# A retention layer and a mixture of experts on one core: the short last chunk as full-array matmuls, and a new order of the first tile

## The chip, the cores and the metric

The kernel runs on one core of one Trainium2 chip. The metric is the device time of one launch in microseconds (us). Most executions of a kernel agree within 0.3%. Every run lists its span and its mean granted TensorE clock, where 1.0 is full speed. A ratio is the mean time of one kernel's fast runs over that of the other's of the same rounds, with a 95% interval, so it is not quite the ratio of the medians that are quoted beside it.

PE is the matmul engine, DVE is VectorE, ACT is ScalarE, POOL is GpSimd, SP is the engine whose queue issues most DMAs. L514 is line 514 of the kernel that was profiled; the two kernels' line numbers differ.

## The reference, cut to what matters

```python
# attention without softmax, per batch (8) and head (8): seq 576, head_dim 64
scores = scale * (q @ k.T)                     # 576 x 576
ret    = scores * gamma[h] ** (i - j)          # for i >= j, else 0
attn   = ret @ v
# x: (8*576, 512) = (4608, 512); then four experts
for e in range(4):
    out += p[:, e:e+1] * (relu(x @ w1[e]) @ w2[e])     # w1: 512x1024, w2: 1024x512
```

576 positions are four chunks of 128 and a short last chunk of 64, called the remainder. The experts take x in nine tiles of 512 rows. Tile 0 holds most of batch 0, tile 1 the remainder of batch 0 and most of batch 1, and so on. While PE works on the experts of tile t, the attention of batch t+1 is woven in between.

## The kernel before

One tile of the experts is a generator. It gives way after each group of matmuls: eight "up" groups of four 512-column matmuls and four "down" groups of eight, for each of four experts, 48 steps numbered from 0. A plan says what attention work follows which step.

```python
def moe(nt, lead=0):
    for e in range(E):
        for fc in range(NFC):                       # 8 up groups
            # for e == 0 and fc < lead: columns 0..255 early, the rest here
            up(ph, e, fc, slice(0, NT)); nc.scalar.activation(hT[:, fc, :], ph, Relu)
            yield
        for ns in range(NSUB):                      # 4 down groups
            ...                                     # po += hT x w2; acc += probs * po
            yield
```

Two heads sit in one pair, on partitions 0 to 63 and 64 to 127. Scores and values of the remainder use two 64x64 corners of the array for each pair:

```python
def Srem(self):
    for p in range(NP):                             # 4 pairs of heads
        for j in (0, 64):
            r = slice(j, j + 64)
            nc.tensor.matmul(s[r, p, :], lhsT=self.qkT[r, 1, p, SM:S], rhs=self.qkT[r, 0, p, SM:S], ...)
# in O_values, if rem: the same loop with lhsT = self.r["v"][r, p, :], rhs = self.sT["r"][r, p, :]
```

The start: after the attention of batch 0, the weights are queued on POOL, and the loads of the remainder and of all later batches stand on SP behind a wait for the first down weights.

```python
load_w1(0, 0); load_w1(0, 1)        # first expert's up weights, in halves, earlier
w20 = load_w2(0)                    # first down weights
for e in range(1, E): load_w1(e); load_w2(e)
load_rem(0, w20)                    # on SP: starts when w20 has landed
load_chunk(1, 0); load_chunk(1, 1)  # and all further loads behind it, in order
```

Batch 1 is transposed on PE in tile 0 (`Tc`, steps 40, 42, 44, 46). From batch 2 on, q and k are transposed by DMA. On SP the loads of batch 2, the four output stores of tile 0 and the ten DMA transposes of batch 2 stand in this order; the transposes read what POOL has cast. The plan for these tiles:

```python
at(7 if nt == 1 else 0, begin)                           # casts, then dmaT(c), then load(b + 1)
at(19 if nt == 1 else 17, lambda: state["A"].S([0, 1]))  # first scores of the next batch
at(24, ... Srem, O_values([0, 1]), kv_all, kv_sum, Srem_mask)
```

## Time and profile before

| | before |
|---|---|
| time, median of the three runs at the start | 561.4 us (560.63 to 562.08) |
| span of the profiled run | 559.2 us |
| PE busy | 98% |
| expert matmuls | 2304 of 512 columns, 216 ns from start to start: 497 us |

PE is the bottleneck, so every pause of PE costs time, unless a later wait of PE becomes shorter by as much. DMA is the second one, for about the first 97 us. The page says so. Its first line gives busy time by engine, the other two lines are 40 equal slices of 14 us: the DMA engines' busy share in tenths, and what they moved.

```profile
PE 545.6 (98%) x3469; PEld 262.5 (47%) x3530; DVE 165.7 (30%) x283; ACT 217.0 (39%) x371; POOL 109.8 (20%) x182
...
DMA  9999999591369025910594058803300100010001
GB/s 232 176 203 200 209 206 231 104 213 15 104 131 180 1 84 89 217 28 38 109 179 92 0 123 157 135 1 98 63 2 1 73 3 0 1 76 0 1 0 75
```

The waits view of PE lists who waited for whom: total us, times, longest.

```profile
PE pt L437 <- POOL qm L427: 2.3, 3, 1.0
PE po L543 <- DMA wt_492<-in_moe_w_dram: 1.7, 1, 1.7
...
PE ph L514 <- DVE xT L329: 0.8, 1, 0.8
```

The first is start-up. The second is the wait for the first down weights at 26 us. The third is the start of tile 1, which needs the last chunk of batch 1.

The timeline of PE in tile 1 has the remainder's scores (start, us, engine, line, count):

```profile
115.02 1.03 PE L514 MATMUL ph<-xT,wt_504 128*128 128x512 bf16 x4
115.97 0.31 PE L336 MATMUL sr<-qkT 64*64 64x64 bf16 x8
116.21 0.64 PE L351 MATMUL o<-sT,vm 128*64 128x128 bf16 x16
```

The last expert matmul of the first line started at 115.66, and the next matmul could have started 216 ns later; it started 309 ns later. Counted the same way, pauses of 92 to 99 ns stand at the changes of the array's form (128x128, 128x64, 64x128, 64x64) in tiles 1 to 6 of this trace. The Trainium skill says that changing the tiling mode drains the engine ("TensorEngine Tiling (Array Packing)", "Key Properties"); it gives no figure, and these 93 ns are one that this case shows.

Last, SP's timeline for the transposes of batch 2 (each with the time its issue took), and PE's timeline for the scores that need them.

```profile
92.28 2.94 SPq L552 DMA_DIRECT2D out_dram<-acc  x4
95.83 1.32 SPq L268 DMA_TRANSPOSE qkT<-qm  x1
...
102.42 1.26 SPq L268 DMA_TRANSPOSE qkT<-km  x1
...
105.04 1.26 SPq L268 DMA_TRANSPOSE qkT<-km  x1
```

```profile
100.54 7.07 PE L514 MATMUL ph<-xT,wt_500 128*128 128x512 bf16 x31
107.55 0.23 PE L276 MATMUL s_1438<-qkT 64*128 64x128 bf16 x1
...
107.72 0.22 PE L276 MATMUL s_1438<-qkT 64*128 64x128 bf16 x1
```

The last k transpose is issued at 105.04 us. The trace's landings of the k transposes before and after it are 2.4 to 2.7 us after their issue, so it lands near 107.5 to 107.7. The first matmul that reads it is the seventh one, at 107.72. PE does not wait there, but it has next to no slack.

### The profile page before, as it was taken

How to read it: one execution, taken by the hardware profiler on the slowest of the kernel's cores; microseconds unless marked ns; L12 is line 12 of the kernel's file. 1: busy time of each engine (PE TensorE's matmuls, PEld its weight loads, DVE VectorE, ACT ScalarE, POOL GpSimd, SP SyncE). 2: the span in 40 equal slices, each digit the busy share in tenths (PEclk: the TensorE clock that was granted, in tenths of full speed). 3: DMA queues.
4: the chain of work that ended last, by engine and by line, in shares of the span. 5: the costliest groups of instructions: out<-in, count | busy, mean ns of one | idle time of the engine just before them, and what ended most of it. 6: DMA issues, size and time to landing. Idle time of an engine off the chain costs nothing.

```text
span 559.2 us, 8453 instructions
## 1 busy us (share of the span) xinstructions
PE 545.6 (98%) x3469; PEld 262.5 (47%) x3530; DVE 165.7 (30%) x283; ACT 217.0 (39%) x371; POOL 109.8 (20%) x182
## 2 busy tenths in 40 slices
PE   7899999999999999999999999999999999999997
PEld 4544455454445444444445444544444444444443
DVE  5402262253214520462035212542046202220222
ACT  6442344433353235323433334323532353335332
POOL 7611247026001520044002600250010000000000
PEclk9999999999999999999999999999999999999999
DMA  9999999591369025910594058803300100010001
GB/s 232 176 203 200 209 206 231 104 213 15 104 131 180 1 84 89 217 28 38 109 179 92 0 123 157 135 1 98 63 2 1 73 3 0 1 76 0 1 0 75
DMA packets 148277, 53.83 MB, mean 96 GB/s; under 512 B 130668, under 2 KB 142188, under 8 KB 148240
## 3 DMA queue, kind: packets, MB, share of 16 engines
q1 hardware_dynamic: 141296, 44.79, 39.2%
q0 software_dynamic: 6800, 8.39, 8.8%
q8 instruction: 27, 0.44, 0.4%
q10 hardware_dynamic: 144, 0.13, 0.1%
q14 instruction: 10, 0.08, 0.1%
HBM read 45.16 MB, written 9.44 MB: 98 GB/s over the span
## 4 chain that ended last, share of the span: by engine, by line
PE 94%; DMA 3%; POOL 1%; issue 1%; SPq 1%; DVE 0%
PE po L543 44%; PE ph L514 43%; DMA wt_492<-in_moe_w_dram 2%; PE o L351 1%; DMA raw_k<-in_k_dram 1%; PE o L365 1%; SPq L85 1%; POOL km L423 0%; PE sr L336 0%; PE orem L358 0%; PE ptc L297 0%; POOL wt_269 L125 0%; PE kvb L389 0%; PE kva L389 0%; PE oc L322 0%
## 5 line engine op out<-in xcount | busy, mean ns | idle before, releaser
L533 ACT ACTIVATE hT<-ph 128x512 bf16<-128x512 f32 x288 | 171.6, 597 | 274.6 <-PE ph L514 274.6
L543 PEld LDWEIGHTS <-hT 128*128 128x128 bf16 x1160 | 112.5, 98 | 134.6 <-DMA wt_492<-in_moe_w_dram 2.2
L549 DVE SCALAR_TENSOR_TENSOR acc<-po,probs,acc 128x512 f32<-128x512 f32 (+1 forms) x109 | 81.3, 746 | 234.6 <-PE po L543 226.8
L514 PE MATMUL ph<-xT,wt_504 128*128 128x512 bf16 x280 | 66.3, 379 | 0.5
L514 PE MATMUL ph<-xT,wt_269 128*128 128x512 bf16 (+1 forms) x303 | 64.2, 362 | 1.4 <-DVE xT L329 0.8
L543 PE MATMUL po<-wt_492,hT 128*128 128x512 bf16 x286 | 63.4, 379 | 1.8 <-DMA wt_492<-in_moe_w_dram 1.7
L543 PE MATMUL po<-wt_506,hT 128*128 128x512 bf16 x273 | 63.8, 379 | 0.8
L514 PE MATMUL ph<-xT,wt_500 128*128 128x512 bf16 x280 | 64.1, 379 | 0.5
L543 PE MATMUL po<-wt_510,hT 128*128 128x512 bf16 (+1 forms) x287 | 63.4, 373 | 0.5
L514 PE MATMUL ph<-xT,wt_508 128*128 128x512 bf16 x286 | 63.7, 379 | 0.2 <-issue 0.2
L543 PE MATMUL po<-wt_502,hT 128*128 128x512 bf16 x280 | 63.4, 379 | 0.4
L403 POOL CAST sbd<-ksum 64x256 bf16<-64x256 f32 x36 | 14.4, 399 | 221.2 <-DVE ksum L408 197.6
L514 PEld LDWEIGHTS <-wt_269 128*128 128x128 bf16 x312 | 30.0, 98 | 32.1 <-issue 0.9
L514 PEld LDWEIGHTS <-wt_508 128*128 128x128 bf16 x288 | 28.0, 98 | 33.3
L514 PEld LDWEIGHTS <-wt_500 128*128 128x128 bf16 x288 | 27.7, 98 | 33.4
L514 PEld LDWEIGHTS <-wt_504 128*128 128x128 bf16 x288 | 26.9, 98 | 30.3
L547 ACT ACTIVATE acc<-po,probs 128x512 f32<-128x512 f32 x36 | 24.7, 687 | 40.1 <-PE po L543 39.1
L235 POOL TENSOR_TENSOR km<-raw_k,gk 128x512 bf16<-128x512 f32 x28 | 29.2, 1043 | 13.9 <-DMA raw_k<-in_k_dram 9.5
L237 POOL CAST vm<-raw_v 128x512 bf16<-128x512 f32 x28 | 17.3, 616 | 41.8 <-PE o L351 34.9
L237 POOL CAST qm<-raw_q 128x512 bf16<-128x512 f32 x28 | 17.1, 611 | 7.4 <-DMA raw_q<-in_q_dram 7.2
L374 DVE TENSOR_TENSOR xT<-o,gq 128x512 bf16<-128x512 f32 x24 | 15.5, 686 | 7.6 <-PE o L365 7.6
L240 POOL TENSOR_TENSOR krb<-raw_kr,gk 64x512 bf16<-64x512 f32 x8 | 8.3, 1037 | 13.8 <-DMA raw_kr<-in_k_dram 13.2
(231 smaller groups left out, 238.7 us busy)
## 6 DMA issues: line engine op xcount, KB each, us to landing
out_dram<-acc SPq DMA_DIRECT2D x35, 256.0 KB, 2.0
raw_k<-in_k_dram SPq DMA_DIRECT2D x32, 256.0 KB, 5.0
raw_q<-in_q_dram SPq DMA_DIRECT2D x32, 256.0 KB, 5.1
raw_v<-in_v_dram SPq DMA_DIRECT2D x32, 256.0 KB, 5.2
wt_269<-in_moe_w_dram POOLq DMA_DIRECT2D x2, 512.0 KB, 5.6
wt_492<-in_moe_w_dram POOLq DMA_DIRECT2D x1, 1024.0 KB, 11.7
wt_500<-in_moe_w_dram POOLq DMA_DIRECT2D x1, 1024.0 KB, 14.5
wt_502<-in_moe_w_dram POOLq DMA_DIRECT2D x1, 1024.0 KB, 20.4
```

The costliest lines, as they stand in the source:

```text
L85: nc.sync.dma_start(out=pairs_of(state[b][n, hf])[:, h], in_=src[b, h, 256 * hf:256 * hf + 256, :].rearrange("h (p j) d -> p h (j d)", j=2))
L235: eng.tensor_tensor(o, i, gk[:, c, :].unsqueeze(2).to_broadcast([128, H, D]), op=MULT)
L237: eng.tensor_copy(o, i)
L240: eng.tensor_tensor(self.r["k"], self.t["kr"], gk[:R, NCH, :].unsqueeze(2).to_broadcast([R, H, D]), op=MULT)
L351: nc.tensor.matmul(o[64 * j:64 * j + 64, c * C:(c + 1) * C], lhsT=self.m["v"][:, c, 2 * p + j, :], rhs=self.sT[p][:, j, c, :], start=(c == ...
L374: nc.vector.tensor_tensor(xT[:, p, b * S:b * S + SM], o, gq[:, p, 0:SM], op=MULT)
L403: eng.tensor_copy(sbd[r, n, :, r], src[r])
L514: nc.tensor.matmul(ph[:, ts], lhsT=w1_sb[e][:, dc, fc * 128:(fc + 1) * 128], rhs=xT[:, dc, n0 + ts.start:n0 + ts.stop], start=(dc == 0), s ...
L533: nc.scalar.activation(hT[:, fc, :], ph, Relu)
L543: nc.tensor.matmul(po, lhsT=hT[:, fc, ns * 128:(ns + 1) * 128], rhs=w2_sb[e][:, fc, d:d + w], start=(fc == 0), stop=(fc == NFC - 1))
L547: nc.scalar.activation(a, po, Copy, scale=pe)
L549: nc.vector.scalar_tensor_tensor(a, po, pe, a, op0=MULT, op1=ADD)
```

## The change

It has two parts. First, the remainder's k (transposed) and v are put into block-diagonal 128x128 operands, so that one full-array matmul does a pair of heads and the array keeps its form. Second, tile 0 runs up 0, up 1, down 0, down 1 instead of up 0, down 0, up 1, down 1, so that the first down weights are needed later; the second expert's up weights are therefore loaded before them, in halves, and the remainder of batch 0 moves to later steps. Some smaller parts go with it: the transposed mixing probabilities move into the start-up, the transposes of batch 1 come one step earlier (39, 41, 43, 45), and tile 1's early part stops at column 384, before the last chunk of batch 1.

```diff
+    kbd = const.tile([128, NP, 128], BF16)          # zeroed once, also the warm-up operand
+    vbd = const.tile([128, NP, 128], BF16)
 # cast_rem
-            for n in ("q", "v"):
-                eng.tensor_copy(self.r[n], self.t[n + "r"])
+            eng.tensor_copy(self.r["q"], self.t["qr"])
+            for j in (0, 64):
+                eng.tensor_copy(vbd[j:j + 64, :, j:j + 64], self.t["vr"][j:j + 64])
+        def put_krem(self, eng, src):
+            for j in (0, 64):
+                eng.tensor_copy(kbd[j:j + 64, :, j:j + 64], src[j:j + 64])
 # Srem
-                for j in (0, 64):
-                    r = slice(j, j + 64)
-                    nc.tensor.matmul(s[r, p, :], lhsT=self.qkT[r, 1, p, SM:S], rhs=self.qkT[r, 0, p, SM:S], ...)
+                nc.tensor.matmul(s[:, p, :], lhsT=kbd[:, p, :], rhs=self.qkT[:, 0, p, SM:S], start=True, stop=True)
 # values of the remainder: from O_values (64x64) to O_states (lhsT=vbd[:, p, :]), next to the state matmuls
 # moe(): ups(e) and downs(e) are generators of their own
+        first = [ups(0), ups(1), downs(0), downs(1)] if nt == 0 else [ups(0), downs(0), ups(1), downs(1)]
-    tiles = [moe(nt, lead=3 if nt < 2 else 0) for nt in range(n_nt)]
+    tiles = [moe(0, lead=3, pause=True), moe(1, lead=2, cut=3 * NT // 4)] + [moe(nt) for nt in range(2, n_nt)]
 # start
+    load_w1(1, 0)
+    load_w1(1, 1)
+    late_constants()
     w20 = load_w2(0)
-    late_constants()
-    for e in range(1, E):
+    load_w2(1)
+    for e in range(2, E):
 # plan of tile 0: remainder of batch 0 at 29, 31, 36 instead of 20, 22, 24
-            for c, g in enumerate((40, 42, 44, 46)):
+            for c, g in enumerate((39, 41, 43, 45)):
 # plan of tiles 1 to 6
+            at(20, lambda: state["A"].put_krem(nc.gpsimd, state["A"].qkT[:, 1, :, SM:S]))
 # ... cut: transposed_probs() split off, ksum with 3 buffers instead of 4, identf earlier; Sc(3), Oc(3) of batch 1
#     moved from behind tile 0 into its plan
```

More of the change, by code (lines that the diff above doesn't have):

```diff
@@ L133 @@
     load_paired(0)
-    warm_in = const.tile([128, 512], BF16)
-    nc.vector.memset(warm_in, 0.0)
+    kbd = const.tile([128, NP, 128], BF16)
+    nc.vector.memset(kbd, 0.0)
     def warm(n):
@@ L139, in warm @@
         for _ in range(n):
-            nc.tensor.matmul(warm_out, lhsT=warm_in[:, 0:128], rhs=warm_in, start=True, stop=True)
+            nc.tensor.matmul(warm_out, lhsT=kbd[:, 0, :], rhs=kbd[:, :, :].rearrange("p a i -> p (a i)"), start=True, stop=True)
     probs_raw = const.tile([NTT, 128, E], FP32)
@@ L156 @@
     make_identity(nc, ident)
+    identf = const.tile([NTT, NTT], FP32)
+    nc.gpsimd.tensor_copy(identf, ident[:NTT, :NTT])
     tri2 = const.tile([128, 2, 128], BF16)
@@ L163 @@
     tri = const.tile([128, 128], BF16)
-    identf = const.tile([NTT, NTT], FP32)
     trir = const.tile([128, R], BF16)
@@ L176, in late_constants @@
                                 base=0, channel_multiplier=-1, pattern=[[1, 128]])
-        nc.gpsimd.tensor_copy(identf, ident[:NTT, :NTT])
     lgp = const.tile([128, NP], FP32)
@@ L199, with transposed_probs @@
     nc.vector.memset(sbd, 0.0)
+    vbd = const.tile([128, NP, 128], BF16)
+    nc.vector.memset(vbd, 0.0)
     probs = const.tile([128, E, NTT], FP32)
     psm = const.tile([128, NTT], FP32)
-    def mixing_weights():
-        pp = ps_at.tile([128, E, NTT], FP32, tag="at", name="pp")
+    def transposed_probs():
+        pp = ps_mm.tile([128, E, NTT], FP32, tag="mm", name="pp")
         for e in range(E):
@@ L207, in mixing_weights @@
         nc.vector.tensor_copy(probs, pp)
+    def mixing_weights():
         nc.vector.tensor_reduce(psm, probs[:, :, :].rearrange("p e t -> p t e"),
@@ L227, in __init__ @@
             self.r = {n: att1.tile([R, H, D], BF16, tag=n + "r", name=n + "rb") for n in "kq"}
-            self.r["v"] = att1.tile([128, NP, D], BF16, tag="vr", name="vrb")
             self.qkT = att1.tile([128, 2, NP, S], BF16, tag="qkT")
@@ L261, in Trem @@
                     nc.tensor.transpose(pt[:, i, p, :], flat(self.r[n][:, 2 * p:2 * p + 2, :]), ident[:R, :R])
-            nc.vector.tensor_copy(self.qkT[:, :, :, SM:S], pt)
+            nc.vector.tensor_copy(self.qkT[:, 0, :, SM:S], pt[:, 0])
+            self.put_krem(nc.vector, pt[:, 1])
+        def put_krem(self, eng, src):
+            for j in (0, 64):
+                eng.tensor_copy(kbd[j:j + 64, :, j:j + 64], src[j:j + 64])
         def dmaT(self, c):
@@ L333, in Srem @@
             for p in range(NP):
-                for j in (0, 64):
-                    r = slice(j, j + 64)
-                    nc.tensor.matmul(s[r, p, :], lhsT=self.qkT[r, 1, p, SM:S], rhs=self.qkT[r, 0, p, SM:S],
-                                     start=True, stop=True, skip_group_check=True)
+                nc.tensor.matmul(s[:, p, :], lhsT=kbd[:, p, :], rhs=self.qkT[:, 0, p, SM:S], start=True, stop=True)
             self.srem = s
@@ L353, in O_values @@
                                          start=(c == 0), stop=False, skip_group_check=True)
-            if rem:
-                for p in range(NP):
-                    for j in (0, 64):
-                        r = slice(j, j + 64)
-                        nc.tensor.matmul(self.orem[r, p, :], lhsT=self.r["v"][r, p, :], rhs=self.sT["r"][r, p, :],
-                                         start=(p == 0), stop=False, skip_group_check=True)
         def O_states(self, pairs, rem=False):
@@ L368, in O_states @@
             if rem:
+                for p in range(NP):
+                    nc.tensor.matmul(self.orem[:, p, :], lhsT=vbd[:, p, :], rhs=self.sT["r"][:, p, :],
+                                     start=(p == 0), stop=False, skip_group_check=True)
                 for n in self.rem_states:
@@ L393, in kv_sum @@
         def kv_sum(self):
-            ksum = att1.tile([128, NCH, NP, D], FP32, tag="ksum", name="ksum")
+            ksum = att1.tile([128, 3, NP, D], FP32, tag="ksum", name="ksum")
             parts = [self.kvp[n // 2][:, n % 2] for n in range(NCH)]
@@ L407, in kv_sum @@
             for n in range(1, NCH):
-                nc.vector.tensor_tensor(ksum[:, n], ksum[:, n - 1], parts[n], op=ADD)
-                put(nc.gpsimd, ksum[:, n], n)
+                nc.vector.tensor_tensor(ksum[:, n % 3], ksum[:, n - 1], parts[n], op=ADD)
+                put(nc.gpsimd, ksum[:, n % 3], n)
     class AttP(Att):
@@ L506, in O, with moe @@
                                         gq[:, 2 * u:2 * u + 2, ts], op=MULT)
-    def moe(nt, lead=0):
+    def moe(nt, lead=0, cut=NT // 2, pause=False):
         n0 = nt * NT
@@ L517, in moe, with ups @@
         acc = [apool.tile([128, Dm], FP32, tag="acc", name="acc") for _ in range(NSUB)]
-        for e in range(E):
-            hT = hpool.tile([128, NFC, NT], BF16, tag="hT")
-            for fc in range(NFC):
-                if e == 0 and fc < lead:
-                    if fc == 0:
-                        early = [ps_mm.tile([128, NT], FP32, tag="mm", name="ph") for _ in range(lead)]
-                        for x in range(lead):
-                            up(early[x], e, x, slice(0, NT // 2))
-                            if x != 1:
-                                yield
+        hTs = {}
+        def ups(e):
+            hT = hTs[e] = hpool.tile([128, NFC, NT], BF16, tag="hT", name="hT")
+            n = lead if e == 0 else 0
+            early = [ps_mm.tile([128, NT], FP32, tag="mm", name="ph") for _ in range(n)]
+            for x in range(n):
+                up(early[x], e, x, slice(0, cut))
+                if pause and x != 1:
+                    yield
+            for fc in range(NFC):
+                if fc < n:
                     ph = early[fc]
-                    up(ph, e, fc, slice(NT // 2, NT))
+                    up(ph, e, fc, slice(cut, NT))
                 else:
@@ L534, in moe, with downs @@
                 yield
+        def downs(e):
+            hT = hTs[e]
             for ns in range(NSUB):
@@ L553, in moe @@
                 yield
+        first = [ups(0), ups(1), downs(0), downs(1)] if nt == 0 else [ups(0), downs(0), ups(1), downs(1)]
+        for stage in first + [g for e in range(2, E) for g in (ups(e), downs(e))]:
+            yield from stage
     a0 = AttP(0)
     UNITS = [(hf, u) for hf in range(2) for u in range(2)]
-    tiles = [moe(nt, lead=3 if nt < 2 else 0) for nt in range(n_nt)]
+    tiles = [moe(0, lead=3, pause=True), moe(1, lead=2, cut=3 * NT // 4)] + [moe(nt) for nt in range(2, n_nt)]
     tile0 = tiles[0]
@@ L581 @@
         a0.kv(hf, u)
+    transposed_probs()
     next(tile0)
@@ L604 @@
             at(3, lambda: a0.cast_rem(nc.gpsimd))
-            at(20, a0.Trem)
-            at(22, a0.Srem, a0.Srem_mask)
-            at(24, a0.Orem)
+            at(29, a0.Trem)
+            at(31, a0.Srem, a0.Srem_mask)
+            at(36, a0.Orem)
             def begin1():
@@ L619 @@
             at(25, begin1)
-            for c, g in enumerate((40, 42, 44, 46)):
+            for c, g in enumerate((39, 41, 43, 45)):
                 at(g, lambda c=c: state["a1"].Tc(c))
-                if c < 3:
-                    at(g + 1, lambda c=c: state["a1"].Sc(c))
+                at(g + 1, lambda c=c: state["a1"].Sc(c))
                 if c > 0:
@@ L626 @@
                 at(g + 1, lambda c=c: state["a1"].kv(c))
+            at(47, lambda: state["a1"].Oc(3))
         elif nt + 1 < B:
@@ L654 @@
                 f()
-        if nt == 0:
-            state["a1"].Sc(3)
-            next(tiles[1])
-            next(tiles[1])
-            state["a1"].Oc(3)
 _INS = ['q', 'k', 'v', 'moe_domain_probs', 'moe_w1', 'moe_w2']
```

## The prediction

> **What bounds the kernel now.** Span 559.2 us. The page gives PE 98% busy, and the chain of work that ended last is 94% PE, nearly all expert matmuls. Their starts in the timeline are 216 ns apart at 512 columns, the warm spacing that the Trainium skill gives ("TensorE: Matmul & The Clock Gate", "Wait — 56ns, not 53.3ns?": 215.7 ns). 2304 of them are about 497 us, so some 62 us are attention, start-up and waits. PE's waits (waits view) are few: 1.7 us for the first down weights (timeline: 26.25 to 27.99), 0.8 us for xT at the start of tile 1, some 2.8 us in the start-up.
>
> **What the change removes, by the timeline's starts.**
> - Short chunk: eight 64x64 matmuls sit between pauses of about 93 ns, paid when PE changes its array form. Amid expert matmuls the scores cost 337 ns; four full-array 64-column ones should cost 4x29 ns (the spacing of the state matmuls now). Estimate: 0.21 us saved for scores and 0.22 for values in batches 0 and 1. In batches 2 to 7 other tiled matmuls are adjacent and one pause remains: 551 to 435 ns for scores, about the same for values: 0.24 us a batch, 1.45 us in all.
> - Tile 0 as up, up, down, down: the 1.74 us wait goes. The second expert's up weights (2 x 2.9 us after 20.4) come just in time; the first down weights then land at 33 to 34 us, where PE needs them at about 33: 0 to 1 us of wait left.
> - Tile 1's early part stops at 384 columns, so it no longer waits for the last chunk of batch 1: 0.78 us. The transposed probabilities fill an idle gap: 0.3 us.
>
> **What it adds.** POOL makes the block-diagonal k copies and one more v copy; it is 20% busy and off the chain.
>
> **Why little of it will arrive.** DMA is saturated to about 97 us (page, slices). The loads of batches 1 and 2 are gated by the first down weights, which now land 5 us later, so this queue loses 5 us of sharing (27 GB/s, the gain of slices 28 to 70 us over 14 to 28): about 0.6 us later. Two places wait for it:
> 1. In tile 0 the transposes of batch 1 come one step earlier, while its chunks land as before (q of chunk 1 at 67.3, of chunk 2 at 71.3 us): 1 to 2 us of new waits.
> 2. In tile 1 the scores of batch 2 start at 107.55 us. Their last DMA transpose is issued at 105.04 and lands, by its neighbours' 2.5 us, at 107.5: no slack. PE should come there 2 to 3 us earlier and wait until about 108.1. What was won before this point is swallowed.
>
> Later tiles have about 5 us of slack there (scores at 165.5, landing 160.5), so their 1.45 us stays. Sum: +0.5 - 1.45, about -1 us.
>
> **Predicted: 560.4 us, 8 in 10 within 558.2 to 561.9. Faster by over 2%: 0.02; within 2%: 0.97; slower: 0.01.**
>
> **What would show it.** Waits view: under 1 us for the first down weights; none for xT at tile 1; new waits for POOL's casts in the transposes of batch 1, and 2 to 3 us for the DMA transposes in the first scores of tile 1. Timeline: short-chunk scores 29 ns apart; tiles 2 to 7 of 59.45 us instead of 59.69.
>
> **What would make it wrong.** If the loads come no later, or the transposes of tile 1 start earlier, up to 5 us arrive (556 us). If PE's clock drops in the new wait, it is slower by about 1 us.

## The result, and the profile after

| | before | after |
|---|---|---|
| median of the first runs | 561.59 us (4 runs) | 560.04 us (559.42 to 561.25, 4 runs) |
| ratio, 95% interval | | 0.9977 (0.9953 to 1.0001) |
| median of a second set, `e12_after_again` | 560.85 us (9 runs) | 559.20 us (5 runs) |
| ratio, 95% interval | | 0.9974 (0.9960 to 0.9988) |
| span of the profiled run | 559.2 us | 557.7 us |

The change is worth about a quarter of a per cent, 1.5 us. The page's first line again: POOL does a little more.

```profile
PE 546.5 (98%) x3462; PEld 261.4 (47%) x3462; DVE 166.9 (30%) x288; ACT 217.5 (39%) x371; POOL 118.6 (21%) x203
```

PE's waits:

```profile
PE s L286 <- DMA qkT<-km: 2.3, 1, 2.3
PE pt L441 <- POOL qm L431: 2.1, 3, 0.8
...
PE ptc L307 <- POOL qm L241: 0.9, 1, 0.9
```

The waits of 1.7 us for weights and 0.8 us for xT are gone. Two new ones are there: 2.3 us for a transposed k, and 0.9 us for a cast. The timeline of the remainder's scores in tile 1:

```profile
114.78 1.03 PE L518 MATMUL ph<-xT,wt 128*128 128x512 bf16 x4
115.65 0.28 PE L344 MATMUL sr<-qkT,kbd 128*128 128x64 bf16 x4
115.86 0.64 PE L358 MATMUL o<-sT,vm 128*64 128x128 bf16 x16
```

From the last expert matmul's start (115.433) to the first value matmul's (115.859) it is now 426 ns; before it was 551. The four scores start 28 to 29 ns apart, right behind the expert matmul. SP and PE at the place that decides:

```profile
92.09 3.01 SPq L561 DMA_DIRECT2D out_dram<-acc  x4
95.72 1.32 SPq L278 DMA_TRANSPOSE qkT<-qm  x1
...
102.31 1.26 SPq L278 DMA_TRANSPOSE qkT<-km  x1
...
104.93 1.26 SPq L278 DMA_TRANSPOSE qkT<-km  x1
```

```profile
103.80 1.03 PE L518 MATMUL ph<-xT,wt 128*128 128x512 bf16 x4
104.75 0.39 PE L286 MATMUL s<-qkT 64*128 64x128 bf16 x6
107.48 0.45 PE L286 MATMUL s<-qkT 64*128 64x128 bf16 x10 [2.34 <-DMA qkT<-km]
```

PE came to these scores at 104.75 instead of 107.55, 2.8 us earlier. Six matmuls could run; the seventh, which needs the last transpose, started at 107.48 instead of 107.72. So 2.8 us were won up to here, and 0.24 us of them were left behind it. The transposes were issued at practically the same times in both kernels (95.83 to 105.04, and 95.72 to 104.93).

After this point the two kernels can be read tile by tile. The first scores of batches 3 to 7 start 59.69 us apart before and 59.44 after, so the full-array form gives 0.25 us a batch. From the seventh matmul to the end of the span it is 451.44 us before and 450.19 after: 1.25 us, which is six batches at 0.25 less 0.26 us that tile 6, with batch 7, gave back between its scores (17.23 us from the first to the second scores, where the tiles before it have 16.96). The trace shows where: the third state matmul of this tile starts at 417.98 us, 307 ns after the second, and what released it is a cast of POOL (`sbd`) at 417.93; the waits view leaves this out, because the modelled end of the matmul before covers most of it. 0.24 and 1.25 make the 1.5 us.

### The profile page after: what moved, and what is told of

It is laid out like the page before. It is cut to its first block, busy times and chain, and to the rows that moved or that the text cites. A ratio compares the mean times of both kernels' runs of the same rounds, so it can differ in the third digit from the quotient of the medians.

```text
span 557.7 us, 8401 instructions
## 1 busy us (share of the span) xinstructions
PE 546.5 (98%) x3462; PEld 261.4 (47%) x3462; DVE 166.9 (30%) x288; ACT 217.5 (39%) x371; POOL 118.6 (21%) x203
## 4 chain that ended last, share of the span: by engine, by line
PE 82%; DMA 11%; SPq 3%; POOL 3%; issue 1%; DVE 0%; POOLq 0%
PE po L552 40%; PE ph L518 37%; DMA raw_v<-in_v_dram 4%; DMA wt<-in_moe_w_dram 2%; DMA raw_vr<-in_v_dram 2%; SPq L278 1%; PE o L358 1%; PE s L286 1%; DMA raw_k<-in_k_dram 1%; DMA raw_q<-in_q_dram 1%; PE o L366 1%; POOL wt L125 1%; SPq L85 1%; DMA qkT<-km 0%; SPq L91 0%
## 5 line engine op out<-in xcount | busy, mean ns | idle before, releaser
L518 PE MATMUL ph<-xT,wt 128*128 128x512 bf16 (+2 forms) x1172 | 260.0, 376 | 0.0
L552 PE MATMUL po<-wt,hT 128*128 128x512 bf16 (+1 forms) x1160 | 255.9, 378 | 0.0
L518 PEld LDWEIGHTS <-wt 128*128 128x128 bf16 x1172 | 111.9, 98 | 127.9
L293 DVE TENSOR_TENSOR sT<-s,tri 128x512 bf16<-128x512 f32 x48 | 29.8, 684 | 115.6 <-PE s L286 115.6
L286 PE MATMUL s<-qkT 64*128 64x128 bf16 x192 | 7.7, 218 | 2.3 <-DMA qkT<-km 2.3
L286 PEld LDWEIGHTS <-qkT 64*128 64x128 bf16 x192 | 5.4, 94 | 7.6 <-issue 5.1
L358 PE MATMUL o<-sT,vm 128*64 128x128 bf16 x192 | 7.6, 222 | 0.0
L248 POOL CAST vbd<-raw_vr 64x256 bf16<-64x256 f32 x16 | 6.4, 398 | 3.4 <-DMA raw_vr<-in_v_dram 3.0
L358 PEld LDWEIGHTS <-vm 128*64 128x64 bf16 x192 | 5.7, 109 | 2.9 <-issue 2.5
L366 PE MATMUL o<-qkT,sbd 128*128 128x128 bf16 x72 | 6.2, 220 | 0.1
```

Of the source, the lines that this page charges most:

```text
L286: nc.tensor.matmul(s[j][:, c, :], lhsT=self.qkT[r, 1, p, cs], rhs=self.qkT[r, 0, p, cs], start=True, stop=True)
L293: nc.vector.tensor_tensor(st[:, j], s[j], tri[:, :].unsqueeze(1).to_broadcast([128, NCH, C]), op=MULT)
L358: nc.tensor.matmul(o[64 * j:64 * j + 64, c * C:(c + 1) * C], lhsT=self.m["v"][:, c, 2 * p + j, :], rhs=self.sT[p][:, j, c, :], start=(c == ...
L518: nc.tensor.matmul(ph[:, ts], lhsT=w1_sb[e][:, dc, fc * 128:(fc + 1) * 128], rhs=xT[:, dc, n0 + ts.start:n0 + ts.stop], start=(dc == 0), s ...
L552: nc.tensor.matmul(po, lhsT=hT[:, fc, ns * 128:(ns + 1) * 128], rhs=w2_sb[e][:, fc, d:d + w], start=(fc == 0), stop=(fc == NFC - 1))
```

## The experiments

Theory 1: what is won before tile 1's first scores is swallowed there, because the transposes of batch 2 land near 107.5 us whatever PE does. Theory 2: the parts of the change are simply worth little, and what the runs show is their sum. A third question is the prediction's own step, that the later gate costs the loads 0.6 us.

The kernel before was run beside each of them. Its median was 561.50 us for e1 to e4, 561.08 for e5 to e8, 561.41 for e9 to e11.

### e1: the changed kernel, tile 1's first scores two steps later

```diff
-            at(19 if nt == 1 else 17, lambda: state["A"].S([0, 1]))
+            at(21 if nt == 1 else 17, lambda: state["A"].S([0, 1]))
```

> The changed kernel with one edit: in tile 1 the first scores of batch 2 stand two down steps later (after step 21 instead of 19). Theory 1 (gains are swallowed by a wait for the DMA transposes, which land near 107.5 us whatever PE does): PE comes to these scores at about 108.2 us, the 2.3 us wait is gone, every later instruction is about 2.3 us earlier, time about 557.7 us, span about 555.3. Theory 2 (the change simply brings only 1.5 us, and the wait would only move to another place): time stays at 560.0.

Measured: 556.66 us (556.55 to 557.02), ratio 0.9914 (0.9901 to 0.9927), span 554.7. PE's timeline:

```profile
104.33 3.62 PE L552 MATMUL po<-wt,hT 128*128 128x512 bf16 x15
107.88 0.62 PE L286 MATMUL s<-qkT 64*128 64x128 bf16 x16
108.43 3.63 PE L552 MATMUL po<-wt,hT 128*128 128x512 bf16 x16
```

Two down groups now fill the time of the wait, all sixteen scores run together, and the span is 2.9 us shorter than that of the changed kernel. From start to start the wait had cost 2.57 us instead of 0.06, that is 2.5 us, and PE was 0.3 us earlier in this run (a wait in tile 0 was 0.6 instead of 0.9 us). There is little room even here: the last transpose was issued at 105.47 us in this run, so by its neighbours' 2.5 us it landed near 108.0, and the seventh score started at 108.06. By the ratios the edit is worth more, 0.6% or 3.4 us; e4 shows what else is in the changed kernel's median. Theory 2 falls: the time was there.

### e2 and e3: each part alone, scores at the old place

e2 is the kernel before with `kbd`, `vbd`, `put_krem` and the two full-array loops of the diff above, and nothing else but what memory asked for (`ksum` with three buffers).

> The kernel before with only the full-array matmuls on block-diagonal k and v (tile 0 in the old order). Saves about 0.43 us in each of batches 0 and 1 before the first scores of tile 1, and 0.25 us a batch after. Theory 1 (pinned at the transposes): the 0.86 us are swallowed by a new wait of about 0.6 us at these scores, total 1.5 to 1.7 us less than before, about 560.0, the same as the whole change. Theory 2 (savings add up): 2.3 us less, about 559.2, and no wait at these scores.

Measured: 560.64 us, ratio 0.9986 (0.9973 to 0.9999). The expectation of 1.5 us less was a little high (0.8 us by the ratio, 1.2 us by the spans), but the wait that it named is there, at 1.18 us instead of 0.6:

```profile
106.30 0.34 PE L283 MATMUL s<-qkT 64*128 64x128 bf16 x6
107.82 0.45 PE L283 MATMUL s<-qkT 64*128 64x128 bf16 x10 [1.18 <-DMA qkT<-km]
```

e3 is the changed kernel with the 64x64 loops of the kernel before put back:

```diff
-                nc.tensor.matmul(s[:, p, :], lhsT=kbd[:, p, :], rhs=self.qkT[:, 0, p, SM:S], start=True, stop=True)
+                for j in (0, 64):
+                    r = slice(j, j + 64)
+                    nc.tensor.matmul(s[r, p, :], lhsT=self.qkT[r, 1, p, SM:S], rhs=self.qkT[r, 0, p, SM:S], ...)
 # and the same for the values; put_krem and vbd go
```

> The changed kernel with the old 64x64 matmuls of the short chunk put back: only the order of tile 0, the weights in halves, the earlier probabilities and tile 1's shorter early part are left. Theory 1: PE comes to the first scores of tile 1 about 2 us earlier than before (near 105.5), waits about 2 us for the transposes, and all is given back: 0 to 0.3 us less than before, about 561.2. Theory 2 (savings add up): 2 us less, about 559.4.

Measured: 560.39 us, ratio 0.9985 (0.9972 to 0.9998). I had expected 561.2. In the profiled run the scores waited too, but earlier:

```profile
104.31 0.34 PE L279 MATMUL s<-qkT 64*128 64x128 bf16 x6
106.10 0.45 PE L279 MATMUL s<-qkT 64*128 64x128 bf16 x10 [1.45 <-DMA qkT<-km]
```

The last transpose was issued at 103.54 in this run, 1.4 us earlier than in the changed kernel, and its weights had come about 1 us earlier from the 25th us on. Some of that is probably luck of one execution: the repeat of the changed kernel (e12) has 103.97 with the same program as 104.93. So the transposes' time varies by 1 us between two executions of one program, and the span follows it. From the seventh score to the end e3 takes 451.43 us, exactly as the kernel before (451.44), and e2 450.18, as the changed kernel (450.19). What differs in front of this point reaches the end only through the landing of the transposes.

### e4: the gate of the loads where it was

```diff
-    load_w1(1, 1)
+    w11 = load_w1(1, 1)
...
-    load_rem(0, w20)
+    load_rem(0, w11)
```

> The changed kernel with the loads of the batch 0 remainder (and all loads queued behind it) gated by the second half of the second expert's up weights (lands 27.4 us) instead of the first down weights (32.5 us). As the prediction had it (a later gate costs the loads about 0.6 us): the last transpose before tile 1's scores lands about 0.6 us earlier, near 106.9, the wait falls from 2.3 to about 1.7 us and the time to about 559.4. Rival (the DMA engines are full either way, and what the loads gain the weights lose): transposes land at 107.5 as before within 0.2 us, the weights end about 1 us later, the time stays at 560.0 within 0.3 us.

Measured: 562.07 us (561.31 to 563.83), ratio 1.0012 (0.9999 to 1.0025): slower than the changed kernel (0.9974), which neither theory had expected. These are the issue and landing times from the traces, in us:

```
                                   before         changed       e4
gate opens (SP's first load)       27.96          32.47         27.26
last weights land                  64.57          63.13         64.18
q of batch 1, chunk 2, lands       71.34          71.21         70.52
raw k of batch 2's remainder       94.14          93.99         93.79
last k transpose issued           105.04         104.93        104.92
```

On the gate the rival is right where it counts: opening it 5.2 us earlier brings the loads 0.7 us at 71 us, costs the weights 1.05 us, and moves the transposes by 0.01 us. This fits engines that are busy either way, where what one queue gets the other lacks. One trace each would be thin evidence, as two executions of one program differ by 1 us at this place, but all profiles together agree. The last k transpose was issued at 105.04 to 105.28 in the kernel before and its variants (e2, e5, e6), at 104.92 and 105.58 with the early gate (e4, e9), and at 103.54 to 105.47, on average 104.5, in the seven with the later gate (e8 is left out). A later gate did not make the transposes later, and the prediction's step fails.

The extra time is somewhere else. The first fence below is PE's timeline at the scores of e4. The second has windows of three us of the same run (length, then busy time by engine), with the granted clock in the third column from the right, and the third has two of these windows in the changed kernel's profiled run.

```profile
104.08 0.29 PE L286 MATMUL s<-qkT 64*128 64x128 bf16 x4
104.92 0.23 PE L286 MATMUL s<-qkT 64*128 64x128 bf16 x2 [0.55 <-DMA qkT<-km]
107.48 0.72 PE L286 MATMUL s<-qkT 64*128 64x128 bf16 x10 [2.34 <-DMA qkT<-km]
```

```profile
104.00:107.00 3.00, 0.60 (x7) 0.21 (x6) 0.00 (x0) 0.60 (x1) 0.00 (x0) 0.96 0.51 103
107.00:110.00 3.00, 2.30 (x14) 1.19 (x16) 2.20 (x4) 0.00 (x0) 0.00 (x0) 0.50 0.22 44
110.00:113.00 3.00, 3.00 (x9) 1.06 (x7) 1.04 (x2) 0.00 (x0) 0.79 (x2) 0.50 1.06 214
113.00:116.00 3.00, 3.00 (x14) 1.23 (x12) 0.75 (x1) 0.00 (x0) 0.00 (x0) 0.90 1.34 223
```

```profile
107.00:110.00 3.00, 2.52 (x20) 1.28 (x21) 2.25 (x4) 0.00 (x0) 0.00 (x0) 1.00 0.22 44
110.00:113.00 3.00, 3.00 (x15) 1.37 (x14) 1.64 (x3) 0.00 (x0) 0.80 (x2) 1.00 1.03 210
```

PE came 0.7 us earlier still, waited 2.9 us in two pieces, and its clock fell to half from 106.8 to 113.6 us. The second scores of tile 1 stand at 125.51 where the changed kernel has 122.55: 3 us lost, with the transposes landing at the same time. So here PE came earlier and ended later.

All six runs of e4 had a mean clock of 0.994 to 0.997. Of the nine runs of the changed kernel (first set and e12) four had 0.996 or 0.997. Their spans average 558.7 us, the other five 557.3. The profiled run of e12 shows the same fall from 107.7 to 111.1 us, after waits of 0.33 and 2.34. The fallen clock is thus part of the changed kernel's median, in about half of its runs. The kernel before has low clocks in five of the 40 runs that are listed with e1 to e12, all on two of the four chips. So have one of the five runs of e5 and one of the six of e11, whose profiles have no wait at these scores; none of these low runs was profiled, so where their clock fell stays open.

The traces also show why one execution keeps its clock and another of the same program loses it. The stretches of half clock last 6.83 us in e4, 3.41 in e12 and 13.65 in e8, which are two, one and four times 3.41 us, and every stretch of full clock is a whole number of 3.41 us too. Cut the span into steps of this length, counted from the clock's first rise: in the step before the fall PE was idle for 2.19 us in e4 and 2.28 in e12 (all 3.41 in e8), and in all 14 profiles no step with 1.74 us of idle time or less is followed by a fall. In the profiled run of the changed kernel a border between two steps cuts the wait of 2.34 us into 1.39 and 0.95. So how the wait lies among these steps is luck, and as far as these profiles show the clock follows that.

### e9: useless matmuls in the wait of e4

If the clock is the cause, work that keeps PE busy in the wait should make e4 faster.

```diff
-            at(19 if nt == 1 else 17, lambda: state["A"].S([0, 1]))
+            at(19 if nt == 1 else 17, *([lambda: warm(8)] if nt == 1 else []), lambda: state["A"].S([0, 1]))
```

> The kernel with the early gate (562.1 us; its profile shows TensorE's granted clock at half speed from about 107 to 114 us, after two waits of 2.9 us together for the transposes, and all six of its runs had a mean clock of 0.994 to 0.997) with eight useless 512-column matmuls before tile 1's first scores, 1.7 us of work into a wait of 2.9. If the slow runs come from the clock that falls in that wait, the clock stays at 0.999 or 1.0 in all runs and the time falls by 2 to 3 us to about 559.5, although work was added. If the clock has nothing to do with it, the time stays at 562.1 or rises.

Measured: 559.93 us, ratio 0.9974 (0.9957 to 0.9992), five of six runs at a clock of 0.999 or 1.0, the sixth at 0.996 with 561.76 us, the longest of them.

```profile
104.37 1.89 PE L141 MATMUL warm_out<-kbd 128*128 128x512 bf16 x8
106.20 0.34 PE L286 MATMUL s<-qkT 64*128 64x128 bf16 x6
108.13 0.45 PE L286 MATMUL s<-qkT 64*128 64x128 bf16 x10 [1.60 <-DMA qkT<-km]
```

```profile
107.00:110.00 3.00, 1.87 (x17) 0.98 (x18) 1.60 (x3) 0.00 (x0) 0.00 (x0) 1.00 0.39 79
```

1.7 us of added work made the kernel about 2 us faster than e4 by the ratios (0.9974 against 1.0012). The clock's part is shown, for e4. It is probably also part of what e1 gained beyond the wait: e1 had no run under 0.999.

### e5, e6, e7: the same parts with the scores two steps later

The edit is that of e1, made to the kernel before (e5), to e2 (e6) and to e3 (e7).

> Control: the kernel before with tile 1's first scores two steps later. Its profile shows no wait at these scores, so theory 1 (the later place only removes the wait for the transposes) expects no gain: within 0.4 us of before, 561.5. If the later place helped for another reason (other neighbours on PE, other PSUM turns), about 3 us would come here too, as in the changed kernel: 558.5.

> Only the full-array matmuls, with tile 1's first scores two steps later, so that nothing can be swallowed there. Theory 1: 0.8 us of batches 0 and 1 now arrive beside the 1.3 to 1.5 us of the later ones: 2.1 to 2.3 us less than before, about 559.3. If the savings of batches 0 and 1 never existed: 1.3 to 1.5 us less, 560.1.

> Only the new order of tile 0 (old 64x64 matmuls), with tile 1's first scores two steps later. Theory 1: the 2.3 us by which PE comes earlier to the end of tile 0 arrive in full: 2 to 2.6 us less than before, about 559.1, against about 560.4 with the scores at their old place. If the order of tile 0 brings nothing of its own: 561.5.

Measured: e5 560.25 us, e6 558.59, e7 557.80. With the others, as ratios to the kernel before:

| | scores at step 19 | scores at step 21 |
|---|---|---|
| kernel before | 1 | 0.9986 (0.9974 to 0.9999), e5 |
| full-array matmuls alone | 0.9986, e2 | 0.9951 (0.9939 to 0.9964), e6 |
| order of tile 0 alone | 0.9985, e3 | 0.9942 (0.9929 to 0.9954), e7 |
| both | 0.9974 (0.9960 to 0.9988), e12 | 0.9914 (0.9901 to 0.9927), e1 |

In the right column the parts add up. Full-array matmuls take 0.35% off (2.0 us of 561), the order of tile 0 takes 0.44% off (2.5 us), both 0.72% (4.0 us, where the sum would be 4.4). In the left column they are worth 0.14, 0.15 and 0.26%. An interval of a ratio is about 0.13% to each side, so single differences are not sharper than some 0.18%.

The control e5 is not quite clean. I had expected no gain within 0.4 us, and its ratio says 0.8 us, with an interval that ends just under 1. In its profiled run the first down weights had landed at 27.13 instead of 27.95 us, and PE was early by as much. In the kernel before, which has no slack at the scores, such luck should be lost to the wait for the transposes; with the scores two steps later it is kept. This is argued, not shown, and it means that up to 0.8 us of e1's gain may belong to the place of the scores alone.

### e8: the stores of tile 0 from another queue

A try at the transposes themselves: SP issues four stores between the loads and the transposes, and they take 3 us of its time.

```diff
-                        eng = nc.scalar if last and d // w % 2 else nc.sync
+                        eng = nc.scalar if nt == 0 or last and d // w % 2 else nc.sync
```

> The changed kernel with the scores at their old place, but the four output stores of tile 0 issued from the ACT queue instead of SP, where they stand between the loads of batch 2 and its transposes (issues 92.1 to 95.1 us). If what holds the transposes is their place in SP's order, they start about 3 us earlier (first issue near 92.8 instead of 95.7), the wait of 2.3 us at tile 1's scores goes and the time falls to about 557. If it is the DMA engines' load (all loads of batch 2 must have landed), they start at most 0.7 us earlier, and the wait stays near 2 us.

Measured: 571.11 us, ratio 1.0183 (1.0169 to 1.0197), with clocks of 0.987 or 0.988. Neither expectation met it. ACT's timeline:

```profile
88.81 0.37 ACTq L561 DMA_DIRECT2D out_dram<-acc  x1
89.24 0.78 ACT L260 ACTIVATE sbd<-kvp 64x256 bf16<-64x256 f32 x2 [16.84 <-DMA raw_v<-in_v_dram]
```

In the built program each DMA waits for the completion of the one eight places before it in one common order. The first three stores were issued at 88.81, 89.98 and 91.19 us, each 0.07 to 0.08 us after the landing of the load of batch 2 that stands eight places before it (88.74, 89.91, 91.11). SP has nothing but DMAs to issue here. ACT also has the evictions of batch 1, they stand behind the store in its program, and it stood still for 16.84 us. PE waited 12.3 us for one of them, and its clock fell again. So e8 does not answer the question that it was made for, whether the order on SP or the load of the DMA engines holds the transposes. The other thirteen profiles speak for the order on SP: in each of them the first transpose is issued 0.60 to 0.62 us after SP has issued the last store, and the last k transpose 9.20 to 9.24 us after the first. What the transposes would do without the stores in front of them stays open.

### e10 and e11: two tries at a better kernel

```diff
-            for c, g in enumerate((39, 41, 43, 45)):
-                at(g, lambda c=c: state["a1"].Tc(c))
+            at(45, lambda: state["a1"].Tc(3))
+            for c, g in enumerate((39, 41, 44, 45)):
+                if c < 3:
+                    at(g, lambda c=c: state["a1"].Tc(c))
 # and the first scores of tile 1 at step 21 (e10) or 22 (e11)
```

> The changed kernel with tile 1's first scores at step 21 and, in tile 0, the transposes of batch 1's chunk 2 one step later (44 instead of 43), beyond the landing of its load. Removes the 0.6 to 0.9 us wait for POOL's cast in tile 0; PE comes to the scores of tile 1 near 107.3 us and may wait some 0.3 us there. Against the same kernel without the second edit (0.9914 of before): 0 to 0.6 us less, about 556.3 if before stands at 561.3.

> As the last one, but tile 1's first scores at step 22, 1.7 us later still. No wait for the transposes is left in any run; but only two steps lie between the scores and the first use of their masked values (step 24), and VectorE's four masks take 2.7 us: PE may wait for them up to 1 us. Expected within 0.5 us of the last one, on either side.

Measured: e10 556.68 us, ratio 0.9910 (0.9895 to 0.9925), span 554.3; e11 556.70 us, ratio 0.9923 (0.9897 to 0.9948). Both are correct, and neither can be told from e1. The 0.6 us wait in tile 0 became one of 0.3 us and one of 0.4 us for a copy of ACT. The simple edit of e1 is what to keep: it is 0.9% faster than the kernel before and about 0.6% faster than the changed one.

### e12: the changed kernel again

> The changed kernel unedited, with more rounds, as the row of the table that the variants are compared with. Expected between 0.996 and 0.999 of before (its first four runs gave 0.9977 with an interval up to 1.0001); some of its runs with a mean clock of 0.994 to 0.997, those about 1 us or more longer than the runs at 0.999 to 1.0, because its wait of about 2.3 us before tile 1's scores is long enough to let the clock fall in some executions.

Measured: 0.9974, as the table above has it, with two of five runs at 0.996 and 0.997. These took 560.27 and 560.11 us, the other three 558.57 to 559.20.

## Why the prediction was right

The time was predicted as 560.4 us and measured as 560.04 (and 559.20 in the second set). Point by point:

- Full-array matmuls: right. Amid expert matmuls the scores cost 337 ns before and 115 now (87.690 to 88.021 less 216), the values with the four state matmuls behind them 463 and 232 ns (batch 1): 0.22 and 0.23 us saved, against 0.21 and 0.22 predicted. In the later batches 0.25 us against 0.24.
- Tile 0: right. PE's wait of 1.74 us for the first down weights is gone from the waits view (what is left is 0.3 us before a weight load of the down matmuls, in the page's groups of instructions; 0 to 1 was predicted), and that for xT is gone.
- Swallowed in tile 1: right, and the heart of it. PE came 2.8 us earlier (2 to 3 predicted) and waited 2.34 us (2 to 3 predicted). e1 took the wait away and found the time.
- New waits in tile 0: right in kind, 0.92 us against 1 to 2.
- "About 0.6 us later" for the loads: wrong. The last transpose was issued 0.11 us earlier, not later. The prediction took the 27 GB/s that the loads gain beside the weights for a free ride. The weights seem to pay for it: their last load landed at 63.13 with the later gate, at 64.18 when e4 put it back, and e4 did not move the transposes. So the term of +0.5 us at the scores measured -0.24.
- The later tiles: -1.45 predicted, -1.25 measured in the profile, for the 0.26 us that tile 6 gave back to a wait for POOL, which the prediction had called off the chain.
- The clock was named as a risk of "about 1 us". It is real. It fell in four of nine runs, at about 1.4 us each, and in all runs of e4.

The two mis-sized terms, -0.7 and +0.2 us, partly cancel, which is why the total looks better than its parts. The fallen clock, which adds some 1.4 us to about half of the runs, also moved the median towards the predicted time. So that it came within 0.4 us is in part luck; the swallowing at tile 1's scores is not.

## What to carry to other kernels

When PE is made faster in a stretch where DMA is full, look for the next place where PE meets a DMA, and read how much slack it has now: a saving in front of it is worth no more than that slack, until the meeting is moved. A wait of PE can cost more than its own length: waits of 2.7 us together (e12) and 2.9 us (e4) halved the clock for 3.4 and 6.8 us after them. Moving real work into the wait was best here (e1), and even useless work paid (e9). Before a DMA is moved to an engine that also computes, look at what the DMA itself waits for.

## What the Trainium skill lacked or had wrong

- "TensorE: Matmul & The Clock Gate", "HAM oscillation — how this bites in real kernels", gives "no PE-idle gaps >~3.4µs" as the rule. Keeping to it was not enough in e4 and e12, where no single wait was longer than 2.34 us: waits of 0.55 and 2.34 us, with two short matmuls between them, brought the clock to half from 106.8 to 113.6 us (e4), and 0.33 and 2.34 us did from 107.7 to 111.1 (e12). One wait of 2.34 us left it at full speed in the profiled run of the changed kernel. What separates these cases is the idle time within one 3.41 us step of the clock: 2.19 us or more before a fall in e4 and e12, 1.74 us or less where none followed.
- "TensorEngine Tiling (Array Packing)", "Key Properties", says that a mode switch drains the engine, without a time. Each switch cost about 93 ns here (309 ns from start to start instead of 216).
- The same page has no measured time for operands as small as these; its "Theoretical Speedup" gives up to 2x where a dimension is 64 or less. Here, with 64 columns, the two 64x64 matmuls of a pair of heads started 3 ns apart and the pairs 31 to 32 ns apart (50 ns once, behind the change of form), while one full-array matmul with half of its weights zero did a pair every 29 ns. Against block-diagonal operands the tiled form gained nothing, before the change of form is counted.
